# Stored orders and slots, a decay column per batch, two norms on VectorE and single q/k blocks in batch 1, in a fused forgetting attention and SwiGLU kernel

## The chip, the core and the metric

The kernel runs on one core of a Trainium2 chip. A core has five engines that run side by side, each with its own queue of instructions in a fixed order: TensorE (PE, matmuls; PEld is its weight load), VectorE (DVE), ScalarE (ACT), GpSimd (POOL) and SyncE (SP, which here only issues DMAs). Engines wait for each other by semaphores. The metric is the device time of one execution in microseconds (us); before the change it is 378.13 us, the median of three runs (377.17 to 379.72).

## The reference

```python
# q, k, v: (8 batches, 8 heads, 576, 64); f: (8, 8, 576)
scores = np.matmul(q, k.transpose(0, 1, 3, 2)) / np.sqrt(D)
cum = np.cumsum(np.log(np.clip(f, 0.0001, 1.0)), axis=-1)
decay = cum[:, :, :, None] - cum[:, :, None, :]
scores = np.where(causal, -1e9, scores + decay)      # causal: strictly above the diagonal
attn = softmax(scores)                                # max subtracted, exp, divided by the sum
x = np.matmul(attn, v)                                # -> x: (4608 tokens, 512), heads side by side
xn = x / np.sqrt(np.mean(x * x, -1) + 1e-6) * rms_g
g, val = xn @ w_gate, xn @ w_val                      # 512 -> 1536
out = (g * sigmoid(g) * val) @ w_out                  # 1536 -> 512
```

## The kernel before

**Attention.** The sequence of 576 is cut into blocks of 128 rows: blocks 0 to 3 and a last block of 64 (index 4, `LAST`). q and k are loaded with a cast to bf16 and turned, so that the head dimension lies on the partitions (`QT`, `KT`). In batches 0 and 1 TensorE turns blocks 0 to 3 (`turn_pe`, lines 454 to 482); everything else is turned by a DMA from SP's queue (`turn`, line 445). TensorE's turning comes in two forms: single blocks, loaded into `qk` (`load_qk`, line 345), with four transposes and a copy of 512 columns for each of q and k; and pairs of blocks, loaded with rows 2p and 2p+1 in partition p into `qk2` (`load_qk2`, line 356), which is a part of the tile `wt`, with sixteen half-width transposes and a copy of 1024 columns. VectorE copies q and ScalarE copies k out of PSUM. Before the change pairs begin at (batch 0, block 1), (1, 0) and (1, 2); blocks (0, 0) and (0, 3) are single.

The decay is not added to the scores: exp(-cum) of the key multiplies v (`scale_v`, line 487: one multiplication of 128x512 on line 495), and the same factor is written as a 65th column of each head's v (line 496, 128x8), so that the product of the exponentials with this column is the softmax's denominator. The rows' own decay cancels. Batches 0 and 1 are scaled on VectorE, batches 2 to 7 on GpSimd, with one instruction of each kind per block.

Scores (line 520) go through ScalarE's exponential (line 538) into `PT`; GpSimd masks the diagonal blocks (line 545). TensorE multiplies with v (line 564), and VectorE divides by the denominator (lines 578 and 580) into `x`.

**Norm.** `norm` (line 587) squares and sums a block on ScalarE (line 596), takes the power -1/2 on GpSimd (lines 600 and 601), and multiplies on ScalarE (line 608). In batch 0 each block has a norm of its own; later two blocks share GpSimd's part. The result is turned by TensorE for groups 0 and 1 (line 616), by DMA for the others.

**SwiGLU.** Tokens come in nine groups of 512: group b holds blocks 0 to 3 of batch b, and the ninth the eight last blocks. `gate` multiplies with the two weights (line 675) and takes the gate by ScalarE's tanh (line 687) and two VectorE instructions (689 and 682). Groups 0 and 1 work in pieces of 128 tokens, the others in 512. The norm's weights `rms_g` multiply group 0's tokens (line 624), and then, once group 0 has used a third of the gate weights, the weights themselves on VectorE (`weigh`, line 387, instruction on line 393: 24 in all). `project` multiplies with w_out in seven products instead of eight (line 729), with sums of quarter blocks before it (lines 705 to 714), sums of the weights once (line 413), and sums of products after it (line 739).

**What sets the order.** The code first builds a list of units (`Plan.add`): an engine, an expected duration, a function that issues the unit's instructions, the units it depends on, and the buffers (`Hold`, a place in a ring) that it takes and gives back. `Plan.run` (line 119) then plays the list through a small simulation at build time: each engine takes, of its units that are ready and whose buffers are free, the one with the lowest key. The keys come from the string `ORDER`, two characters per unit in the order of adding. Instructions are issued in the order of this simulation, so each engine's queue is fixed; on the chip semaphores hold each instruction until its inputs and its buffer are ready.

Loads of q, k, v and weights are issued from GpSimd's queue (v of block (0, 0), f and `rms_g` from SP's). Lines named below: 298 builds the identity matrix on GpSimd, 351 and 374 issue loads, 479 copies turned q and k.

Of the kernel before, what the change touches and what calls it, by code (L numbers as in the profile page):

```python
# [12 lines left out]
ALU = mybir.AluOpType  # L13
# [3 lines left out]


XPE, DT1, WIDE1 = 2, 0, 0
BASE = -18.8  # L20
VA, NA = 1, 1.2
LETTERS = string.digits + string.ascii_letters
ORDER = (
    "0e1q020d000b0c080j0406030i0a0u0w0l0m0q0r0x090o0E0H0I070p010h050g0f0t0k0y0n0J0s0O0v0T0F1b0K1e0A0W0P1h"
    "0X1u151S1a241y2p2S3o3l44111I1k2g1Z2U1L2E1U2K2d2Z1B2z2n392O3k3s4q323K3h3Z2M3j5s6a373P3w4r404Q3C4z2v3d"
    "3U4J484Y4i59585N4B5m5w6h6O72555G4w5g7c7p4P5y5i627A7M5d5T5L6n7m7B5S6A5X6J7E7Q6Z7d9w9L8l8D828q7T8k8H8Z"
    "8W9c7J7V8P969M9Z7O869C9SaLaWb8boaOb2cHcUcMd2cBcQbpbNaGaPbdbyaUb9bjbDb0bhbubTcectbWcaeoeDeteMexeUe8el"
    "edeqeieAeFf1ePfceHf8hXigifiziliJi3iphSi7iCiPgXh8h1hegPgZhahrh6hkgUh3hphChIhUhshJjijzj7jljCjNjejsjtjG"
    "jHjRkIkTkEkPkNkVlhlFl1lelllTl9lul7lqldly0z0C0B0D0M0G0N0S0L0Q0R0V0U131d191f141i1r1l1s1x1F17181j1z1v1C"
    "1G1N1W27222820262D2L3a2V2T343c2Y383g3u3G2N3p3A3H3v3N3S424c3x4a4j4e4t4x4H4W3I4b4A50454S525b5v5D5F4f4G"  # L30
    "3z3W7g5I5U5P5Y6365474s4L5a6G4Z5t3r3F6x666k6r6e5h5K5r67756s6z6S6K6U71767h5J6C6B7i7t7f8a818o8v8Q9a606V"
    "5B6q8591989i9q9ya25R6Q6j788z6b6X6L7x9g9E9K9R9N7e7U777L8b9Ua1a5a4adaiaoaB7v8ja9aj9oaSaZbabqbEbxbO8J8Y"
    "8T9h9WbMbXc5c7ccck9A9O8f8wataeaq8y8OamcrcEcScybfbwbIc4bGdgdldAdxdKdOdRdVdfdsdndzd4dYebe4eCeKeRf0c6cq"
    "b4bkc0eZf7fdfGfLfPbsbVbZcldhcgcucLcYdofSfXg2g1eVflf6frfgg6gfgkgbgmgqgtgyeyeNeJf5eSgEgHgMh4hhhwhKfhfx"
    "fEfRfohWi2ieirixiHiBiViRj6iZiLj2iqiEjojKjPjVjThohEhyhPhgk2kdkik7kpktkvkyhOi5hHhZhzkBkMkHlvlClSlXhYij"
    "i8iwismcmjmpmsmxmBjSkfjAk1k0jMkajZkjk8mJmVn2mOl8lkkYlalrn9ninnnenrnwnznCm1mdlzlMm9nOnTnVocojoLoQlRm5"
    "lJm0lOp0p6papgpipm0Y100Z121m1o1p1A1M1O1P1T2l2q2r2w3m3t3L3Q464m4l4y4K4R4O535E5M5V646c6i6m6u7I7P7S808e"
    "8i8n8u8A8G8I8N8S8V979f9m9u9s9zaaafaganaQaVaXb1b3bbbibnbBbHbKbQcFcNcOcTd5dcdddidDdIdLdPefejeIeOeWf2f4"
    "fbfefjfufzfWfZgageggglhbhfhjhmhqhxi1i6iaidiiiniGiMiTj1jbjklmlsltlxlAlElLlQlZm4mkmomrmumvmCmQmUmWn0nN"
    "nQogokooosoIoMoZp5p4pbpcpjphpnpqpupPpT161c1g1n1t1K1Q1V1Y211X232f2C2G2A2H2Q2X336E7W8h8r8K3Y4E4I4T5157"  # L40
    "4X545l5f696f6t6M6T6o6v6D878s8F939l8B8X949d9j9x9n9t9G9r9D9I9Va3ac9T9Ya7auc8chcxcKb5brbAbPcpcDbJbRcfc1"
    "cXd0d9dudEd6dbdkdpdvdCdFdMdUeYfafkfqfCfpfyfKftfDfJfTg0g9fOfUg4gjgpgxgAgJhnhDi9iDiYjdiojhjyitiQiUj5jn"
    "jJj0j8jjjqjxjDjEk6lHlWm6mamfmqmhmmmwmAmFmImMmPmYmTmXn6n5n8nbnfnoomoRoUp2p9pkoYp3pdpfpppspwpApFpzpEpJ"
    "pWq0q4q9qh1w1E1D1H1J252c2a2e2k2P3E2W313M4h4v4o4D4M4p5c1R2o2b2h2u292i2j2m2s353f3b3e3n3i3y3q3B3T3D6F2t"
    "2I2y2B2R2x302F2J363R43494d4k3J3V3O3X4g707G5e5A5k5u5H5p615z5W6l747n7a7r7y6H6Y6P6W7b5j795q5x7k7N8g7Y89"
# [31 lines left out]
class Plan:  # L77
# [3 lines left out]
    def __init__(self, rings, fifo):  # L81
        self.units, self.fifo = [], fifo
        self.free = {name: list(range(n)) for name, n in rings.items()}
        self.left = {name: [] for name in rings}

    def add(self, eng, dur, key, emit, deps=(), take=(), give=(), lat=0.04):
        u = Unit(eng, dur, key, emit, lat)
        for h in take:
            if h not in self.left[h.ring]:
                self.left[h.ring].append(h)  # L90
# [96 lines left out]
def fox_ffn_kernel(ctx, tc, q, k, v, f, moe_w_gate, moe_w_val, moe_w_out, moe_rms_g, out):  # L187
# [134 lines left out]
    EARLY = 3  # L322
# [516 lines left out]
```

## Time and profile before

| | |
|---|---|
| median of three runs | 378.13 us (377.17 to 379.72) |
| the profiled execution: device time, span | 376.9 us, 375.2 us |
| TensorE's granted clock, mean | 0.997 |
| busy: PE, DVE, ACT, POOL | 348.3, 290.9, 225.9, 207.5 us |
| weight loads (PEld) | 244.9 us |
| data moved by DMA | 44.87 MB in 133479 packets |

The span runs from the first to the last instruction; the device time has a little around it. Busy times are of one engine, and engines overlap. A row of a timeline or of a group begins with the engine and the line of the kernel, then the operation and its output and inputs; `x24` is a count. A wait is told as "engine line <- engine line that ended it: us in total, times, longest". Rows of a stage begin with the stretch and its length. An instruction's duration runs until it has finished, so a stretched one has stood still for a part of it.

### The profile page before, as it was taken

To read this page: it belongs to the slowest core of one execution; us is meant where nothing else is said; L and a number is where in the kernel's file an instruction comes from. 1 tells how busy PE (TensorE), PEld (TensorE's weight loads), DVE (VectorE), ACT (ScalarE), POOL (GpSimd) and SP (SyncE) were. 2 spreads that over 40 slices of the span, in tenths; PEclk is the share of its full clock that TensorE was granted. 3 is DMA by queue.
4 is the path that set the end of the run, shared out by engine and by line. 5 is a ranking of instruction groups with operands and counts; after the bars stand their busy time and mean duration, and the time that the engine had idled before them with its cause. 6 is when DMAs were issued, how large, how long until landed. Compare 5 with 4: busy or idle time off the path is not lost. (4 is left out here: it accounts for less than half of the span.)

```text
span 375.2 us, 10418 instructions
## 1 busy us (share of the span) xinstructions
PE 348.3 (93%) x4266; PEld 244.9 (65%) x4266; DVE 290.9 (78%) x542; ACT 225.9 (60%) x360; POOL 207.5 (55%) x280
## 2 busy tenths in 40 slices
PE   1799887988999999999999998999999999999994
PEld 1689876978987557755545676556646694445683
DVE  5578997999884868677588887787876976889673
ACT  5696667772897786568957645478833735333210
POOL 8986856899898996775497775842300210000000
PEclk9999999999999999999999999999999999999998
DMA  9999999999999999299199995993201132000015
GB/s 145 214 201 229 181 146 151 168 126 223 170 113 169 185 168 128 67 204 114 33 144 120 162 175 135 143 158 54 40 27 45 41 95 85 0 0 2 28 64 133
DMA packets 133479, 44.87 MB, mean 120 GB/s; under 512 B 117300, under 2 KB 131128, under 8 KB 133432
## 3 DMA queue, kind: packets, MB, share of 16 engines
q0 software_dynamic: 76368, 23.34, 60.7%
q1 hardware_dynamic: 57064, 20.87, 33.1%
q8 instruction: 33, 0.54, 0.6%
q14 instruction: 14, 0.11, 0.1%
HBM read 37.90 MB, written 9.44 MB: 126 GB/s over the span
## 5 line engine op out<-in xcount | busy, mean ns | idle before, releaser
L687 ACT ACTIVATE th<-ff 128x512 f32<-128x512 f32 x108 | 63.9, 596 | 75.8 <-PE ff L675 73.9
L538 ACT ACTIVATE PT<-sc 128x1024 bf16<-128x1024 f32 x96 | 94.8, 1019 | 18.3 <-PE sc L520 16.1
L675 PE MATMUL ff<-xT,wg 128*128 128x128 bf16 (+1 forms) x672 | 96.2, 289 | 3.0 <-DVE hT L682 1.6
L675 PE MATMUL ff<-xT,wv 128*128 128x128 bf16 (+1 forms) x672 | 96.4, 288 | 2.3 <-DVE ores L739 1.2
L689 DVE SCALAR_TENSOR_TENSOR ga<-th,ff 128x512 f32<-128x512 f32 x108 | 73.5, 684 | 25.9 <-ACT th L687 22.4
L682 DVE SCALAR_TENSOR_TENSOR hT<-ga,ff 128x512 bf16<-128x512 f32 x108 | 72.8, 684 | 15.5 <-PE ff L675 13.8
L675 PEld LDWEIGHTS <-wg 128*128 128x128 bf16 x720 | 54.0, 98 | 36.3 <-issue 3.1
L675 PEld LDWEIGHTS <-wv 128*128 128x128 bf16 x720 | 52.8, 98 | 36.3 <-issue 2.5
L545 POOL TENSOR_SCALAR_AFFINE_SELECT PT<-PT 128x1024 bf16<-128x1024 bf16 x32 | 36.0, 1124 | 52.7 <-ACT PT L538 52.6
L729 PEld LDWEIGHTS <-hT 128*128 128x128 bf16 x432 | 41.4, 98 | 7.3 <-issue 0.2
L564 PEld LDWEIGHTS <-PT 128*128 128x128 bf16 x896 | 38.0, 99 | 11.5 <-issue 1.6
L564 PE MATMUL ff<-Vs,PT 128*128 128x65 bf16 x896 | 42.3, 195 | 2.1 <-POOL PT L545 0.7
L739 DVE TENSOR_TENSOR ores<-ores,ff 128x512 f32<-128x512 f32 x45 | 30.6, 684 | 17.0 <-PE ff L729 12.9
L729 PE MATMUL ff<-wo,hT 128*128 128x256 bf16 x324 | 39.5, 273 | 0.0
L495 POOL TENSOR_TENSOR Vs<-v,decT 128x512 bf16<-128x512 f32 (+1 forms) x30 | 31.7, 1057 | 10.2 <-DMA v<-in_v_dram 6.6
L520 PE MATMUL sc<-QT,KT 64*128 64x128 bf16 (+1 forms) x960 | 34.1, 213 | 2.3 <-ACT PT L538 1.7
L580 DVE TENSOR_TENSOR x<-ff,rden 128x256 f32<-128x256 f32 (+1 forms) x80 | 33.8, 423 | 2.8
L608 ACT ACTIVATE xn<-x,rs 128x512 bf16<-128x512 f32 (+1 forms) x40 | 27.8, 719 | 13.0 <-POOL rs L601 12.9
L374 POOL DMA_DIRECT2D v<-in_v_dram x39 | 34.6, 888 | 1.8 <-DVE hT L682 1.0
L729 PEld LDWEIGHTS <-sm 128*128 128x128 bf16 x324 | 30.9, 98 | 6.7 <-issue 2.0
L520 PEld LDWEIGHTS <-KT 64*128 64x128 bf16 x960 | 24.5, 96 | 14.4 <-issue 12.5
L351 POOL DMA_DIRECT2D qk<-in_k_dram x34 | 29.6, 879 | 4.5 <-DMA wo<-in_moe_w_out_dram 3.4
(74 smaller groups left out, 351.7 us busy)
## 6 DMA issues: line engine op xcount, KB each, us to landing
out_dram<-ores SPq DMA_DIRECT2D x32, 256.0 KB, 2.6
v<-in_v_dram POOLq DMA_DIRECT2D x31, 256.0 KB, 6.6
qk<-in_k_dram POOLq DMA_DIRECT2D x26, 128.0 KB, 6.7
qk<-in_q_dram POOLq DMA_DIRECT2D x26, 128.0 KB, 6.0
wg<-in_moe_w_gate_dram POOLq DMA_DIRECT2D x3, 512.0 KB, 10.7
wv<-in_moe_w_val_dram POOLq DMA_DIRECT2D x3, 512.0 KB, 13.1
wo<-in_moe_w_out_dram POOLq DMA_DIRECT2D x2, 768.0 KB, 12.1
v<-in_v_dram POOLq DMA_DIRECT2D x8, 128.0 KB, 6.8
```

The source lines that it names most:

```text
L374: queue.dma_start(out=T_v32[h.slot][0:n, :, :], in_=v[b, :, p0:p0 + n, :].rearrange("h p d -> p h d"))
L495: eng.tensor_tensor(T_Vs[hv.slot][0:n, j, :, 0:D], T_v32[h.slot][0:n, :, :], bcast(dj, D), ALU.mult)
L520: nc.tensor.matmul(t[:, par, c:c + n], lhsT=kt[r, p, kj * 128:(kj + 1) * 128], rhs=qt[r, p, qi * 128:qi * 128 + n], start=True, stop=True)
L538: nc.scalar.activation(T_of_p[hp.slot][:, 0:2 * half].rearrange("p (a c) -> p a c", a=2)[:, :, 0:cols], T_sc[h.slot][:, :, 0:cols], ACT.Ex ...
L545: nc.gpsimd.affine_select(out=d, in_=d, pattern=[[0, 8], [1, n]], compare_op=ALU.is_ge, fill=0.0, base=0, channel_multiplier=-1)
L564: nc.tensor.matmul(po[:, p, :], lhsT=T_of_p[h.slot][:, c:c + 128], rhs=vs[:, kj, 2 * p + par, :], start=(kj == 0), stop=(kj == qi))
L580: nc.vector.tensor_tensor(d, po[:, :, 0:D], bcast(r, D), ALU.mult)
L675: nc.tensor.matmul(T_ff[h.slot][:, c:c + n], lhsT=w[:, dc, fc * 128:(fc + 1) * 128], rhs=xT[:, dc, t0:t0 + n], start=(dc == 0), stop=(dc = ...
L682: nc.vector.scalar_tensor_tensor(hT, in0=three[0], scalar=0.5, in1=three[1], op0=ALU.mult, op1=ALU.mult)
L687: th = act(0.6, key - 0.1, lambda: nc.scalar.activation(T_th[ht.slot], T_ff[hg.slot], ACT.Tanh, scale=0.5), [ug], take=[ht])
L689: a = dve(0.69, key - 0.1, lambda: nc.vector.scalar_tensor_tensor(T_ga[ha.slot], in0=T_th[ht.slot], scalar=1.0, in1=T_ff[hg.slot], op0=ALU ...
L729: nc.tensor.matmul(t[:, s * HD:(s + 1) * HD], lhsT=a()[:, fc, s * 128:(s + 1) * 128], rhs=w[:, fc, :], start=(not more and s == 0 and fc = ...
```

## The change

- `Plan.run` no longer simulates. `ORDER` is now a full ranking of the units over all engines, and a second string, `SLOTS`, gives each buffer's place in its ring. [...] `run` sorts the units by rank and asserts that dependencies and buffers are respected; which waits an engine has still follows from the order and the slots.
- The decay column (line 496) stays as it was for batch 0. For batches 1 to 7 it is one GpSimd instruction per batch, of 128 partitions by 5 blocks by 8 heads, instead of one per block; the values (line 564) depend on it as well.
- The norms of blocks (0, 0) and (0, 1) have their square with its sum, and their multiplication, on VectorE instead of ScalarE. The power between them stays on GpSimd. The buffer `xn` of these two is taken at the square, whose output goes there.
- Blocks (1, 2) and (1, 3) are loaded and turned as single blocks, not as a pair.
- Some expected durations in the units differ; they no longer have an effect, since nothing is simulated. `COPY_DVE` is empty, and the condition on the gates' width (`g < 2`) gives the same groups as before.

```diff
-XPE, DT1, WIDE1 = 2, 0, 0
+XPE = 2
+PAIRS = {(0, 1), (1, 0)}
+NORM_DVE = {(0, 0), (0, 1)}
+COPY_DVE = set()
 ORDER = (
-    "0e1q020d000b0c080j0406030i0a0u0w0l0m0q0r0x090o0E0H0I070p010h050g0f0t0k0y0n0J0s0O0v0T0F1b0K1e0A0W0P1h"
...
+    "000102030a0j06050b090c070g0h0v0z0o0p0s0t0A0d0l0M0W0U0f0q0i0u040e080k0m0x0D110n0G0y0Y0w0S0N1k0I15101C"
...
+SLOTS = (
+    "12301120000132014372632143570512533110656813567a42470b603923321550723224214461031877302176215a0b5309"
...
     def run(self):
...
+        for h, c in zip(self.holds, SLOTS):
+            h.slot = LETTERS.index(c)
+        ranks = [LETTERS.index(a) * len(LETTERS) + LETTERS.index(b) for a, b in zip(ORDER[::2], ORDER[1::2])]
...
+        order = [u for _, u in sorted(zip(ranks, self.units), key=lambda x: x[0])]
...
     for j in (0, 2):
-        if DT1 * 2 > 3 - j:
+        if (1, j) not in PAIRS:
             for i in (j, j + 1):
                 load_qk(1, i, -9.5 + i * 0.1)
...
         def emit(eng):
...
             eng.tensor_tensor(T_Vs[hv.slot][0:n, j, :, 0:D], T_v32[h.slot][0:n, :, :], bcast(dj, D), ALU.mult)
-            eng.tensor_copy(T_Vs[hv.slot][0:n, j, :, D], dj)
+            if b == 0:
+                eng.tensor_copy(T_Vs[hv.slot][0:n, j, :, D], dj)
...
+        if b > 0 and j == 0:
+            column[b] = pool(0.25, key, lambda: nc.gpsimd.tensor_copy(
+                T_Vs[hv.slot][:, :, :, D], decT[:, :, b * H:(b + 1) * H]), [L_dec], take=[hv])
+        scaled[b, j] = us + [column[b]] if b > 0 else us
...
     def norm(b, js, key):
...
+                if on_dve:
+                    nc.vector.scalar_tensor_tensor(T_xn[hn.slot][0:n, :], in0=x, scalar=1.0, in1=x, op0=ALU.mult,
+                                                   op1=ALU.mult, accum_out=sq[:, i:i + 1])
+                    return
...
-                nc.scalar.mul(T_xn[hn.slot][0:n, :], T_x[hx.slot][0:n, :], rs[:, i:i + 1])
+                mul = nc.vector.tensor_scalar_mul if on_dve else nc.scalar.mul
+                mul(T_xn[hn.slot][0:n, :], T_x[hx.slot][0:n, :], rs[:, i:i + 1])
...
-        if b >= 2 or qi == LAST or (b == 1 and qi >= 4 - 2 * DT1):
+        if b >= 2 or qi == LAST:
             turn(b, qi, qkey(b, qi) - 0.25)
-        elif (b, qi) in {(0, 0), (0, 1), (0, 3), (1, 0), (1, 2)}:
-            turn_pe(b, qi, (b, qi) in {(0, 1), (1, 0), (1, 2)}, qkey(b, qi) - 0.25)
+        elif (b, qi - 1) not in PAIRS:
+            turn_pe(b, qi, (b, qi) in PAIRS, qkey(b, qi) - 0.25)
```

More of the change, by code (lines that the diff above doesn't have):

```diff
@@ L77, with __init__ @@
 class Plan:
[L81 to L84, printed above, removed]
+    def __init__(self, rings):
+        self.units, self.rings, self.holds = [], rings, []
     def add(self, eng, dur, key, emit, deps=(), take=(), give=(), lat=0.04):
@@ L489, in scale_v @@
         h, hv = hold_v[b, j], hold_Vs[b]
+        early = b == 0 and j < EARLY
         def emit(eng):
```

223 lines of the change are left out of this document (90 added, 133 removed).

## The prediction

> **What bounds the kernel now.** I read the page first, then the engines' busy time by stage, then what TensorE waited for, then single lines where the stage named an engine.
>
> ```profile
> span 375.2 us, 10418 instructions
> ...
> PE   1799887988999999999999998999999999999994
> ...
> PE 39%; DVE 2%; issue 0%; DVEq 0%
> ```
>
> The chain of waits that ended last covers only the final 41% of the span and is nearly all TensorE (39%); the slices of PE show dents in the first ten slices (some 100 us) and again near the 24th. So late work is matmul after matmul, and what can be won lies early. Busy time by stage says where:
>
> ```profile
> core 0: us, PE busy (x) PEld busy (x) DVE busy (x) ACT busy (x) POOL busy (x), PEclk, DMA share, GB/s
> 0.00:10.00 10.00, 2.27 (x22) 1.97 (x22) 5.02 (x25) 4.81 (x6) 8.80 (x17) 1.00 1.23 151
> 10.00:30.00 20.00, 17.24 (x295) 15.09 (x292) 13.33 (x31) 17.16 (x25) 17.43 (x23) 1.00 1.41 205
> 30.00:110.00 80.00, 71.22 (x1396) 65.93 (x1393) 74.47 (x147) 53.38 (x83) 63.66 (x83) 1.00 1.57 169
> 110.00:200.00 90.00, 89.34 (x1013) 54.52 (x1012) 65.26 (x127) 68.34 (x111) 69.14 (x93) 1.00 1.15 135
> 200.00:240.00 40.00, 38.26 (x418) 26.04 (x416) 31.82 (x47) 22.84 (x36) 31.50 (x41) 1.00 1.18 147
> 240.00:360.00 120.00, 120.00 (x1046) 72.63 (x1045) 93.90 (x161) 58.20 (x99) 17.00 (x27) 1.00 0.26 51
> 360.00:375.20 15.20, 9.96 (x92) 8.68 (x89) 7.14 (x10) 1.17 (x2) 0.00 (x0) 0.92 0.39 104
> ```
>
> TensorE's idle time, stage by stage (length less PE busy): 7.73 before 10 us, 2.76 to 30, 8.78 to 110, 0.66 to 200, 1.74 to 240, none to 360, 5.24 in the tail. The first is mostly loads and the tail is the last sum and its store; neither is work the change takes away. What a better order can reach is 2.76 + 8.78 + 0.66 + 1.74 = 13.9 us. From 30 to 110 us VectorE is busy 74.47 of 80, more than any other engine: it is the bound there. From 10 to 30 ScalarE (17.16) and GpSimd (17.43) are the busy ones and VectorE has 6.67 free. TensorE's waits agree:
>
> ```profile
> PE ff L464 <- DVE ident L299: 7.7, 1, 7.7
> PE ff L616 <- ACT xn L608: 2.7, 3, 2.3
> PE ff L675 <- DVE hT L682: 2.2, 3, 0.9
> PE sc L520 <- ACT PT L538: 1.7, 2, 1.3
> ```
>
> After the first matmul the longest are on ScalarE's norm and exponentials, then on VectorE's gate outputs.
>
> **The change part by part.** *1. Order and the shared port.* The columns of the first two rows are shortest/median/longest ns:
>
> ```profile
> L393 DVE TENSOR_SCALAR wg<-wg,rgT x12: 330/350/1760, 45.9 to 86.3; 128x512 bf16<-128x512 bf16 x12
> L393 DVE TENSOR_SCALAR wv<-wv,rgT x12: 334/437/2286, 63.5 to 92.8; 128x512 bf16<-128x512 bf16 x12
> ```
> ```profile
> 30.00:110.00 80.00, 13.33 (x24) 1.00 1.57 169
> ```
> ```profile
> 79.27 0.98 POOL L374 DMA_DIRECT2D v<-in_v_dram  x1
> 80.26 1.11 POOL L545 TENSOR_SCALAR_AFFINE_SELECT PT<-PT 128x1024 bf16<-128x1024 bf16 x1
> ...
> 78.13 3.61 DVE L393 TENSOR_SCALAR wv<-wv,rgT 128x512 bf16<-128x512 bf16 x3
> ```
>
> The 24 weight scalings of line 393 took 13.33 us, all inside the bound stage. At the shortest, 0.33, they would take 7.9: 5.4 us are stretch. Three of them fill 3.61 us where 1.0 would do, and GpSimd works all through it (the issue at 79.27, the mask from 80.26). The other stretched line there is the scaling of v:
>
> ```profile
> L495 DVE TENSOR_TENSOR Vs<-v,decT x7: 683/692/2281, 19.9 to 87.1; 128x512 bf16<-128x512 f32 x5, 64x512 bf16<-64x512 f32 x2
> ```
> ```profile
> 30.00:110.00 80.00, 6.96 (x6) 9.54 (x9) 1.00 1.57 169
> ```
>
> Six took 6.96 us (first busy column); six medians are 4.15, so 2.8 are stretch. Together 8.2 us of the bound engine in its stage. The stored order can win between nothing and all of it. I take two thirds, 5.5: the medians of line 393 (0.35, 0.44) show that half of them run unstretched already, so there is room to place them.
>
> [...]
>
> *2. Decay column.*
>
> ```profile
> L496 POOL CAST Vs<-decT x30: 208/221/982, 77.8 to 252.1; 128x8 bf16<-128x8 f32 x24, 64x8 bf16<-64x8 f32 x6
> L496 DVE CAST Vs<-decT x7: 173/181/368, 20.5 to 88.1; 128x8 bf16<-128x8 f32 x5, 64x8 bf16<-64x8 f32 x2
> ```
>
> Five casts of batch 1 leave VectorE: 5 x 0.18 = 0.9 us. On GpSimd 30 casts go and 7 come, of 40 elements instead of 8; between 0.21 and 0.98 each by the row, nearer 0.22 as the size hardly shows there. GpSimd is not TensorE's wait, so I count nothing for that. The new column instruction waits for the batch's Vs buffer, and behind it in GpSimd's queue stand load issues; but the scaling of block 0 has waited for the same buffer at the same place, except in batch 1, whose buffer is free from the start.
>
> *3. Single blocks in batch 1.*
>
> ```profile
> L479 DVE COPY QT<-ff x5: 414/1284/1302, 8.3 to 42.3; 128x1024 bf16<-128x1024 bf16 x3, 128x512 bf16<-128x512 bf16 x2
> ```
> ```profile
> L351 POOL DMA_DIRECT2D qk<-in_k_dram x34: 687/906/1099, 1.3 to 237.5; - x34
> ```
>
> One copy of 1.30 becomes two of 0.41 on VectorE: 0.5 less, and ScalarE's K copy likewise. TensorE's 32 half-width transposes become 16 full ones, which I count as equal. Two loads become four: two more issues, 1.8 us on GpSimd's queue, with the last loads of batches 0 and 1 and the output weights behind them. GpSimd is free 16.3 us in that stage, so between 0 and +1.8; I take +0.2.
>
> VectorE thus gets 5.5 + 0.9 + 0.5 = 6.9 us back between 30 and 110. TensorE cannot get back more than its 8.78 idle, and some VectorE time freed will stand as VectorE idle (5.53 already does); at four fifths the term is -5.5.
>
> *4. Two norms on VectorE.*
>
> ```profile
> L689 DVE SCALAR_TENSOR_TENSOR ga<-th,ff 128x512 f32<-128x512 f32 x108 | 73.5, 684 | 25.9 <-ACT th L687 22.4
> ...
> L608 ACT ACTIVATE xn<-x,rs 128x512 bf16<-128x512 f32 x32 | 22.0, 720 | 7.4 <-POOL rs L601 7.2
> L596 ACT ACTIVATE junk<-x 128x512 bf16<-128x512 f32 x32 | 20.2, 631 | 6.1 <-DVE x L580 5.9
> ```
>
> ScalarE loses 2 x (0.63 + 0.72) = 2.7 us between 10 and 30, where it is nearly full. VectorE gains two squares (0.68 by line 689, the same operation) and two multiplies, shown nowhere: between 0.33 (line 393 in 16 bit) and 0.72 (line 608); I take 0.45, the input being twice as wide as line 393's. That is 2.3 us, in the 6.67 that VectorE has free, so nothing if the wait for GpSimd's power lies beside other work (rival C if it doesn't). TensorE's idle there is 2.76, and the waits on line 608 and on the exponentials, 4.4 us over the run, belong largely to this stage. I take -1.0, between 0 and -2.76.
>
> *5. The first loads.* Two characters in the stored string are a unit's rank, in the order in which units are added. The issues of q and k of block (0,0) are units 26 and 28, that of the pair's q is unit 32. Their keys were 07, 01 and 0f; their ranks are now 0f, 0i and 08. So GpSimd issues the pair's q first, then q, then k; before it was k, q, pair.
>
> ```profile
> 1.31 1.10 POOL L351 DMA_DIRECT2D qk<-in_k_dram  x1 [0.81 <-POOLq L823]
> 2.41 0.90 POOL L351 DMA_DIRECT2D qk<-in_q_dram  x1
> ```
> ```profile
> 9.59 0.61 PE L520 MATMUL sc<-QT,KT 64*128 64x128 bf16 x8
> ```
> ```profile
> DMA to landing us min/median/max: 4.0/5.1/7.8
> ```
>
> k goes out 1.10 + 0.90 = 2.0 us later, at 3.31, and lands (third row: time to landing of these loads before 10 us) between 7.3 and 11.1; with transposes and copy, about 1 us, the first scores could begin anywhere from no later than now, 9.59, to 12.1: +0 to +2.5. Against that the identity, made on GpSimd by line 298, now comes behind five load issues instead of six, 0.9 earlier, and TensorE's first wait, 7.7, was for it: -0.5 at best. I take +0.3, near the short end, since the pair's transposes fill the time.
>
> *6. 200 to 240 us.*
>
> ```profile
> L708 DVE TENSOR_TENSOR hT<-hT x9: 945/953/1832, 70.1 to 361.3; 128x1536 bf16<-128x1536 bf16 x9
> ```
>
> The sums of the seven-product scheme stretch from 0.95 to as much as 1.83, and TensorE's idle is 1.74. I take -0.8, between 0 and -1.7.
>
> Everything else (slots stored instead of handed out by the planner, the planner's own durations) issues no instruction. Sum: -5.5 - 1.0 - 0.8 + 0.2 + 0.3 = -6.8 us. The profiled execution took 376.9 us (span 375.2 and 1.7 around it), so it would take 370.1; the median of the runs is 378.13, 1.2 above, and the forecast is for such a median: 378.1 - 6.8 = **371.3**.
>
> **The rivals.** A difference under 1% (3.8 us) can't be told from none.
>
> *B, no change.* The stretch moves instead of going: GpSimd is busy 63.66 and VectorE 74.47 of the same 80 us, so their sum is 138, and they must overlap for at least 58 us whatever the order. Many VectorE instructions are never stretched (line 689's mean of 684 hardly leaves room), which speaks against it; that GpSimd's loads cannot wait speaks for it. Then parts 2 to 5 alone remain: four fifths of 1.4, the 1.0 of the norms, less 0.5, so -1.6 and 376.5.
>
> *C, slower.* The norms' multiplies now stand in VectorE's queue waiting for GpSimd's power, and what is queued behind them (evacuation of attention values, copies of Q, gates) waits too, and TensorE and ScalarE with it.
>
> ```profile
> ACT xn L608 <- POOL rs L601: 12.9, 10, 2.5
> ```
>
> ScalarE lost up to 2.5 us in one such wait. Two of them on VectorE are 5.0 us between 10 and 30, passed on whole if nothing else was placed between square and multiply; it decides once the two exceed VectorE's slack at that point. With the port's gain eaten: 378.1 + 5.0 = 383. Against it: the free 6.67.
>
> *D, the loads held up.* If the two multiplies keep GpSimd from issuing, its queue, 17.43 of 20 us full, slips by up to 2 x 0.72 = 1.4 and the norms' gain of 1.0 is lost: 371.3 + 2.4 = 373.7. No issue in the row of line 351 was stretched past 1.10, though line 393 ran beside many, so the trace speaks against it.
>
> [...]
>
> **How the numbers follow.** Forecast 0.55, B 0.25, C 0.13, D 0.07. The forecast's bounds: at best all 13.9 us of reachable idle less a little, 378.1 - 13.6 = 364.5; at the other end, a third of the port's gain and k late by 2.5 gives about 376. The range 364.5 to 380 leaves out most of C and a few per cent on the fast side. Faster by over 1% means under 374.3: forecast and D, 0.62. Within 1%: B, 0.25. Slower: C, 0.13.
>
> **What would show it.** Line 393's 24 scalings near 8 to 9 us instead of 13.33, and line 495 on VectorE near 0.69 each. TensorE's idle between 30 and 110 at 3 to 4 us instead of 8.78. Line 608's share on VectorE, with a wait on GpSimd's power well under 1 us; a wait of 2 would mean C. First scores between 9 and 10.5 us. The forecast is wrong if line 393 is short and TensorE's idle stays: then another engine was the bound.

## The result, and the profile after

Measured side by side, the changed kernel takes 0.9866 of the time of the kernel before, with a 95% interval of 0.9825 to 0.9907: 378.13 x 0.9866 = 373.1 us, where 371.3 was forecast. The comparison takes only executions within 1.5% of the fastest of the same kernel, which here are 7 of 20 of the changed kernel and all 20 of the kernel before; over all 20 the medians are 379.42 us after and 379.61 before. So the changed kernel reaches the gain in a part of its executions only, and its median shows none: it runs from 372.64 to 383.74 us, the kernel before from 377.03 to 382.26.

Two executions of the changed kernel were profiled. The first took 378.31 us, the second 373.24. This is the page of the second, in the order of the lines shown of before (the span; busy time by engine; the slices of TensorE, its granted clock and DMA; the chain of waits):

```profile
span 371.5 us, 10375 instructions
...
PE 346.8 (93%) x4250; PEld 244.2 (66%) x4250; DVE 282.9 (76%) x544; ACT 223.7 (60%) x355; POOL 205.8 (55%) x259
...
PE   0789988799999999999999999999999999999993
...
PEclk9969999999999999999999999999999999999999
DMA  9999999999999999399999954991100341000024
...
PE 85%; POOL 6%; DVE 4%; issue 2%; ACT 2%; POOLq 0%; DVEq 0%; ACTq 0%
```

The dents near the 24th slice are gone, those in the first ten are not, and the clock row has a 6 that was not there before. Busy time by stage, same execution (columns as in the prediction):

```profile
0.00:10.00 10.00, 1.13 (x12) 1.04 (x14) 5.13 (x23) 4.31 (x6) 8.79 (x15) 1.00 1.30 155
10.00:30.00 20.00, 16.18 (x274) 13.91 (x271) 15.28 (x37) 13.46 (x16) 18.28 (x24) 0.83 1.34 216
30.00:110.00 80.00, 74.15 (x1454) 69.00 (x1452) 69.90 (x144) 56.35 (x92) 63.52 (x80) 1.00 1.65 163
110.00:200.00 90.00, 89.78 (x1021) 54.40 (x1019) 65.65 (x130) 70.04 (x112) 77.00 (x94) 1.00 1.29 154
200.00:240.00 40.00, 40.00 (x422) 27.73 (x420) 30.36 (x54) 21.59 (x35) 21.52 (x27) 1.00 0.86 130
240.00:360.00 120.00, 120.00 (x1033) 73.33 (x1032) 93.10 (x155) 57.38 (x96) 16.74 (x23) 1.00 0.22 48
360.00:371.50 11.50, 5.59 (x52) 4.77 (x49) 3.44 (x5) 0.58 (x1) 0.00 (x0) 0.97 0.39 92
```

TensorE's idle time (length less PE busy), beside that of before and the forecast:

| stage | before | after | difference | forecast |
|---|---|---|---|---|
| 0 to 10 | 7.73 | 8.87 | +1.1 | +0.3 (first loads) |
| 10 to 30 | 2.76 | 3.82 | +1.1 | -1.0 (norms) |
| 30 to 110 | 8.78 | 5.85 | -2.9 | -5.3 (port, column, blocks) |
| 110 to 200 | 0.66 | 0.22 | -0.4 | 0 |
| 200 to 240 | 1.74 | 0.00 | -1.7 | -0.8 (sums) |
| after 360 | 5.24 | 5.91 | +0.7 | 0 |
| TensorE's busy time | 348.3 | 346.8 | -1.5 | 0 |
| span | 375.2 | 371.5 | -3.7 | -6.8 |

So two stages gave time and the first 30 us took some back. Idle time does not hold what a lower clock costs: in the first profile, of span 376.6 us, sixteen score matmuls of one shape (line 482) take 1.04 us from 22.14 us on, at a granted clock of 0.50, and 0.62 us from 26.51 on, at 1.00. The stage from 10 to 30 us has a clock of 0.83, and in the second profile 274 matmuls, where before it had 1.00 and 295. The first profile, 5.1 us longer, has the same start and loses most of the rest in one place:

```profile
span 376.6 us, 10345 instructions
```
```profile
30.00:110.00 80.00, 71.25 (x1354) 66.11 (x1350) 71.00 (x136) 52.17 (x83) 58.77 (x74) 0.98 1.59 162
```

There TensorE is idle 8.75 us between 30 and 110, as before the change (8.78).

**The scalings and GpSimd.** The 24 weight scalings (now line 347), first in the execution of 371.5, then in that of 376.6; shortest/median/longest ns, and all 24 in the stage as the first busy column:

```profile
L347 DVE TENSOR_SCALAR wg<-wg,rgT x12: 333/345/1627, 43.4 to 82.6; 128x512 bf16<-128x512 bf16 x12
L347 DVE TENSOR_SCALAR wv<-wv,rgT x12: 333/344/765, 58.0 to 88.7; 128x512 bf16<-128x512 bf16 x12
```
```profile
30.00:110.00 80.00, 9.95 (x24) 1.00 1.65 163
```
```profile
L347 DVE TENSOR_SCALAR wg<-wg,rgT x12: 334/344/2122, 43.4 to 81.0; 128x512 bf16<-128x512 bf16 x12
L347 DVE TENSOR_SCALAR wv<-wv,rgT x12: 333/346/3980, 57.9 to 89.4; 128x512 bf16<-128x512 bf16 x12
```
```profile
30.00:110.00 80.00, 15.48 (x24) 0.98 1.59 162
```

13.33 us became 9.95 in the one and 15.48 in the other. The long one of 3.98 us is seen in the timeline of VectorE and GpSimd (start, length), and TensorE's longest waits of that execution say who paid:

```profile
86.72 6.65 DVE L347 TENSOR_SCALAR wv<-wv,rgT 128x512 bf16<-128x512 bf16 x3
...
88.21 2.16 POOL L453 TENSOR_TENSOR Vs<-v,decT 128x512 bf16<-128x512 f32 x2
90.31 0.93 POOL L328 DMA_DIRECT2D v<-in_v_dram  x1
91.24 0.90 POOL L305 DMA_DIRECT2D qk<-in_k_dram  x1
92.13 1.08 POOL L453 TENSOR_TENSOR Vs<-v,decT 64x512 bf16<-64x512 f32 x1
93.13 0.46 POOL L460 CAST Vs<-decT 128x40 bf16<-128x40 f32 x1
```
```profile
PE ff L646 <- DVE wv L347: 4.4, 2, 3.7
```

Three scalings fill 6.65 us where 1.0 would do. The last starts at 89.4 and ends at 93.4; from 89.2 to 93.2 GpSimd runs four instructions in a row (a scaling of v, two issues of loads, a scaling of v) and then begins a fifth. TensorE waits 3.7 us for it. In the execution of 371.5 no wait of TensorE on line 347 is listed. The stall costs more than itself, by windows of the first profile (the number after the five busy columns is the granted clock):

```profile
90.00:92.00 2.00, 0.00 (x0) 0.00 (x0) 2.00 (x1) 0.00 (x0) 2.00 (x3) 1.00 1.01 186
92.00:94.00 2.00, 0.57 (x9) 0.58 (x10) 2.00 (x3) 0.00 (x0) 2.00 (x4) 0.96 1.09 178
94.00:96.00 2.00, 2.00 (x21) 2.00 (x20) 1.79 (x3) 0.60 (x1) 2.00 (x3) 0.50 0.79 47
96.00:98.00 2.00, 2.00 (x28) 2.00 (x26) 0.84 (x2) 0.22 (x1) 2.00 (x3) 0.68 1.27 89
98.00:100.00 2.00, 2.00 (x40) 2.00 (x38) 1.29 (x2) 0.81 (x2) 2.00 (x4) 1.00 1.66 112
```

For some 4 us the clock is at 0.50 to 0.68, and TensorE, busy throughout with matmuls of one shape (line 646), does 21 and 28 where 40 go from 98 us on, at 1.00. Just before that it did next to nothing, from 89.8 to 93.4. Between 10 and 30 us of the same kernel the clock is lower too (0.83 over the stage), with a longest gap of TensorE there of 1.55 us in this execution and 1.66 in that of 371.5; what lowers it there isn't shown.

The other operations counted as stretched went as hoped: the scaling of v on VectorE (line 453) and the sums (line 679), both from the execution of 371.5:

```profile
L453 DVE TENSOR_TENSOR Vs<-v,decT x7: 676/685/1033, 22.4 to 74.3; 128x512 bf16<-128x512 f32 x5, 64x512 bf16<-64x512 f32 x2
...
L679 DVE TENSOR_TENSOR hT<-hT x9: 941/948/952, 67.4 to 358.0; 128x1536 bf16<-128x1536 bf16 x9
```

The longest were 2.28 and 1.83 us before, and are 1.03 and 0.95 now.

**The start.** Timeline of the changed kernel (execution of 371.5), and below it the same two first lines of an experiment that sets the first loads' order back (it is told below):

```profile
6.97 1.35 DVE L263 TENSOR_TENSOR_SCAN hT<-one,hT 64x576 f32<-64x576 f32 x1 [0.67 <-ACT hT L257]
7.10 1.31 POOL masks.py:199 TENSOR_SCALAR_AFFINE_SELECT ident_f<-ident_f 128x128 f32<-128x128 f32 x1
...
8.87 1.01 PE L418 MATMUL ff<-ident,qk 128*128 128x128 bf16 x8 [8.87 <-DVE ident L253]
...
10.81 0.61 PE L482 MATMUL sc<-QT,KT 64*128 64x128 bf16 x8
```
```profile
5.19 1.35 DVE L263 TENSOR_TENSOR_SCAN hT<-one,hT 64x576 f32<-64x576 f32 x1 [0.67 <-ACT hT L257]
...
7.09 0.29 POOL masks.py:199 TENSOR_SCALAR_AFFINE_SELECT ident_f<-ident_f 128x128 f32<-128x128 f32 x1
```

The stored order issues v before f on SP's queue. So the scan over f comes 1.8 us later and meets GpSimd's instruction that makes the identity, which takes 1.31 us instead of 0.29. TensorE's first matmul starts at 8.87 instead of 7.73, the first scores at 10.81 instead of 9.59. How much the order of the loads costs differs between executions: in six experiments with the same first loads the scan starts between 6.08 and 6.32, the instruction that it meets takes 0.42 to 0.55 us, and the first matmul starts at 7.98 to 8.22. Between 10 and 30 the granted clock is 0.83, where it was 1.00; the late start alone is not shown to be the cause, since of two of those experiments the one that starts at 8.22 (the column per block) keeps 1.00 and the one that starts at 7.98 (the norms on ScalarE) has 0.83.

**The norms.** Multiplication on VectorE, and what it waited for between 10 and 30 us, execution of 376.6:

```profile
L579 DVE TENSOR_SCALAR xn<-x,rs x2: 486/512/537, 21.0 to 24.6; 128x512 bf16<-128x512 f32 x2
```

```profile
DVE xn L579 <- POOL rs L571: 0.6, 1, 0.6
```

It took 0.51 us (0.45 was assumed), and only one of the two waited for GpSimd's power, 0.6 us.

### The profile page after: what moved, and what is told of

It reads as the page before. It is cut to its first block, busy times and chain, and to the rows that moved or that the text cites. A ratio compares the mean times of both kernels' runs of the same rounds, so it can differ in the third digit from the quotient of the medians.

```text
span 376.6 us, 10345 instructions
## 1 busy us (share of the span) xinstructions
PE 348.2 (92%) x4220; PEld 246.6 (65%) x4250; DVE 288.2 (77%) x544; ACT 224.0 (59%) x355; POOL 206.5 (55%) x259
## 2 busy tenths in 40 slices
DMA packets 135561, 44.88 MB, mean 119 GB/s; under 512 B 119381, under 2 KB 133209, under 8 KB 135513
## 4 chain that ended last, share of the span: by engine, by line
PE 79%; POOL 7%; DVE 5%; DMA 4%; issue 3%; ACT 1%; POOLq 0%; ACTq 0%; DVEq 0%
PE ff L646 44%; PE ff L700 20%; PE ff L526 8%; PE sc L482 6%; DMA qk<-in_k_dram 4%; DVE wv L347 2%; POOL PT L507 2%; POOL qk L305 1%; DVE ga L660 1%; ACT PT L500 1%; POOL wt L317 1%; DVE x L542 1%; POOL v L328 1%; POOL Vs L453 0%; POOL rs L571 0%
## 5 line engine op out<-in xcount | busy, mean ns | idle before, releaser
L646 PE MATMUL ff<-xT,wg 128*128 128x128 bf16 (+1 forms) x655 | 95.1, 289 | 0.6
L646 PEld LDWEIGHTS <-wv 128*128 128x128 bf16 x720 | 54.6, 99 | 40.6 <-DVE wv L347 4.7
L507 POOL TENSOR_SCALAR_AFFINE_SELECT PT<-PT 128x1024 bf16<-128x1024 bf16 x32 | 39.1, 1222 | 53.9 <-ACT PT L500 50.7
L579 ACT ACTIVATE xn<-x,rs 128x512 bf16<-128x512 f32 (+1 forms) x38 | 26.3, 718 | 11.2 <-POOL rs L571 11.2
L305 POOL DMA_DIRECT2D qk<-in_q_dram x36 | 31.3, 871 | 0.0
```

What stands on the lines that cost most here:

```text
L305: nc.gpsimd.dma_start(out=T_qk[h.slot][0:n, :].rearrange("p (h d) -> p h d", d=D), in_=src[b, :, p0:p0 + n, :].rearrange("h p d -> p h d"))
L507: nc.gpsimd.affine_select(out=d, in_=d, pattern=[[0, 8], [1, n]], compare_op=ALU.is_ge, fill=0.0, base=0, channel_multiplier=-1)
L646: nc.tensor.matmul(T_ff[h.slot][:, c:c + n], lhsT=w[:, dc, fc * 128:(fc + 1) * 128], rhs=xT[:, dc, t0:t0 + n], start=(dc == 0), stop=(dc = ...
```

## The experiments

The theory after the result: the gain comes from the stored order and slots; it is smaller than forecast since VectorE's busy time between 30 and 110 us is worth less than the four fifths assumed; and where it is absent, a weight scaling is held by GpSimd (the port theory of the expectations: the runs show the holding, and none shows a port). The rivals: VectorE is the bound and the stretch alone decides; the late start decides; the norms or the column took the gain back. Ratios are to the kernel before, run in turn on the same chip, with 95% intervals.

**The same kernel again.** No edit.

> The changed kernel unaltered, for its own spread and for comparison with the three beside it. Its 20 executions so far lie between 372.64 and 383.74 us. Port theory: the spread is made by where GpSimd's instructions happen to fall against the weight scalings of line 347; so this profile again shows one or more scalings far above their shortest 0.33 us, and TensorE waits on line 347 by about the same amount. Rival (late data, or the granted clock): the 24 scalings add up to much the same whatever the time, and the slower executions show a lower clock or later landings.

0.9885 (0.9812 to 0.9958), six executions from 373.24 to 383.24 us. The result stands, and so does the spread. The profile of 371.5 above is from here: a short execution, in which TensorE doesn't wait on the scalings. Their sum, 9.95 us against 15.48 in the long one, is not the same whatever the time, as the rival had it.

**Kernel before, without the weight scalings.**

```diff
-                    nc.vector.tensor_scalar_mul(w[:, dc, c0:c1], w[:, dc, c0:c1], rgT[:, dc:dc + 1])
+                    pass
```

> The kernel before with the 24 weight scalings of line 393 left out, so that the gate products use weights without rms_g for groups 1 to 8; nothing else differs. VectorE loses 13.33 us of its 74.47 between 30 and 110 us. This measures the conversion that the forecast set at four fifths. If VectorE is the bound of that stage as forecast, four fifths of 13.33 is more than the 8.78 us that TensorE is idle there, so nearly all of the idle would go: idle at about 1 us, time 379 - 8 = 371. If the planner's fixed order and the loads set the end as well (rival: the freed time stands as VectorE idle), idle falls by less than half: 5 or more stays, and the time is 375 or above.

1.0014 (0.9974 to 1.0053), median 379.74 us. 13.33 us of work leave VectorE, and the time does not move. The conversion of four fifths falls, and with it the reading that VectorE is the bound of this stage. Where the freed time went isn't known: the execution that was profiled took 1239 us, for reasons its trace doesn't show, and says nothing on this. The kernel leaves out the norm's weights for groups 1 to 8.

**Kernel before, weight scalings on ScalarE.**

```diff
-                    nc.vector.tensor_scalar_mul(w[:, dc, c0:c1], w[:, dc, c0:c1], rgT[:, dc:dc + 1])
-            Lw[nm, i] = [dve(2.0, key, emit, deps[nm])]
+                    nc.scalar.mul(w[:, dc, c0:c1], w[:, dc, c0:c1], rgT[:, dc:dc + 1])
+            Lw[nm, i] = [act(2.0, key, emit, deps[nm])]
```

> The same move in the kernel before the change (planner and all else as before): what the stretched scalings cost there. Port theory, as the prediction had it: 5.4 us of stretch and 7.9 us of work leave the engine that bounds the stage from 30 to 110 us, so 3 to 6 us less, 372 to 376. Rival (the stretch was hidden, or ScalarE becomes the bound): within 1.5 us of the kernel before.

1.0057 (1.0023 to 1.009). Its stage row:

```profile
30.00:110.00 80.00, 72.17 (x1362) 64.88 (x1360) 60.41 (x119) 66.11 (x106) 59.49 (x79) 0.98 1.75 165
```

VectorE fell from 74.47 to 60.41 us, and TensorE's idle from 8.78 to 7.83 only: 14 us for 1. ScalarE took on 13 us in exchange, so this alone would not be clean; with the experiment above it says the same. TensorE's longest waits of this stage are now 2.8 us for a gate output of VectorE and 2.4 for GpSimd's mask: as one wait went, others came.

**Changed kernel, weight scalings on ScalarE.** The same edit.

> The 24 weight scalings of the changed kernel are made on ScalarE, in the same place of the global order. [...] Port theory: about 24 x 0.7 = 17 us more on ScalarE, VectorE freed of 8 to 15 us, no stretch, time 370 to 374 and spread under 4 us. Rival: ScalarE's exponentials and gates are delayed by 1.5 to 3 us at each of the six groups and TensorE waits for them instead: no faster than the changed kernel, 376 to 382.

1.0146 (1.0089 to 1.0203), the slowest of all. TensorE's longest waits between 10 and 110 us:

```profile
PE sc L482 <- ACT PT L500: 5.8, 4, 3.0
PE ff L418 <- ACT KT L436: 3.9, 1, 3.9
```

None of the 24 is stretched on ScalarE (707 to 722 ns). But a fixed order made for other engines doesn't bear such a move: the exponentials and the copy of K now stand behind the scalings, for which the stored order had left no place.

**Changed kernel, weight scalings in a form that also writes a sum.** The same product, plus zero, with its sum written to a spare column:

```diff
-                    nc.vector.tensor_scalar_mul(w[:, dc, c0:c1], w[:, dc, c0:c1], rgT[:, dc:dc + 1])
+                    nc.vector.tensor_scalar(w[:, dc, c0:c1], in0=w[:, dc, c0:c1], scalar1=rgT[:, dc:dc + 1],
+                                            op0=ALU.mult, scalar2=0.0, op1=ALU.add, accum_out=spare[:, 0:1])
```

> The 24 weight scalings stay on VectorE in the same places, but as an instruction that also writes a sum (to a spare column), which by the port theory does not take the port shared with GpSimd. Port theory: each takes 0.6 to 0.7 us, none is stretched beyond 0.8, so 24 take 14 to 16 us, TensorE's wait on this line (4.4 us in the profile of the changed kernel) goes below 1, and the times lie between 371 and 376 with a spread under 4 us. Rival: GpSimd is not what holds them; the extra 6 us of work on VectorE (0.25 more for each) come on top, 380 or more, and the spread stays.

0.9968 (0.9939 to 0.9997); all 12 executions between 375.55 and 380.38 us.

```profile
L348 DVE TENSOR_SCALAR_CACHE_REDUCE wg<-wg,rgT x12: 729/746/747, 42.6 to 83.0; 128x512 bf16<-128x512 bf16 x12
...
L348 DVE TENSOR_SCALAR_CACHE_REDUCE wv<-wv,rgT x12: 728/746/747, 58.5 to 90.7; 128x512 bf16<-128x512 bf16 x12
```
```profile
30.00:110.00 80.00, 71.69 (x1390) 66.59 (x1387) 73.52 (x164) 54.45 (x86) 62.28 (x77) 1.00 1.67 164
```

None of the 24 is stretched in this profile. The last four run one after the other from 88.30 to 91.40 us beside the same row of GpSimd instructions (88.14 to 93.32) that held line 347 for 3.98 us: what stretches line 347 goes with GpSimd's instructions and with the form of the scaling (3.98 us in the one, 0.73 to 0.75 in the other), and not with its inputs or its queue; by what way GpSimd holds it isn't shown. The price is 0.75 instead of 0.34 us, and 0.08 for reading the sum, which begins just before the scaling ends. The 24 scalings with their 24 readings:

```profile
30.00:110.00 80.00, 18.03 (x48) 1.00 1.67 164
```

That is 8.1 us more than the 9.95 of the execution of 371.5, for a span 2.3 us longer. By these two executions 1 us of VectorE was worth about 0.3; by the ratios (0.9968 against 0.9866, 3.9 us) about 0.5. The times that the port theory gave (371 to 376 us) did not come: without the stretch, but with the dearer form, the short times are nearly gone, and so are those above 380.4.

**Only two of the six groups of scalings in that form,** those that were stretched most, the first third of wg and the last of wv (3.1 and 6.9 us for four in the execution of 376.6, where the four from 57.92 us on take 1.1):

```diff
+ONE_PORT = {("g", 0), ("v", 2)}
...
+                    if (nm, i) in ONE_PORT:
+                        nc.vector.tensor_scalar(w[:, dc, c0:c1], in0=w[:, dc, c0:c1], scalar1=rgT[:, dc:dc + 1],
+                                                op0=ALU.mult, scalar2=0.0, op1=ALU.add, accum_out=spare[:, 0:1])
+                        continue
```

> [...] Port theory: the slower group of times (378 to 384) goes, the faster (372 to 377) stays: 372 to 377 for nearly all runs, ratio to the kernel before 0.985 to 0.99. Rival: the slower times come from elsewhere (landings, clock): about 6 in 10 runs stay above 378.

0.9846 (0.9798 to 0.9895): 371.66, 372.63, 373.31, 374.38, 375.71 and 382.54 us. By ratio this can't be told from the changed kernel; what differs is how often the short time is reached: five of six executions here lie under 376 us, against 6 of the 20 first ones of the changed kernel and 1 of the 6 above. The case of 382.54 us shows another stall, told below.

**The first loads in the old order.** The ranks of the loads of f and of the first v are exchanged:

```diff
-    "000102030a0j06050b090c070g0h0v0z0o0p0s0t0A0d0l0M0W0U0f0q0i0u040e080k0m0x0D110n0G0y0Y0w0S0N1k0I15101C"
+    "00010203040j06050b090c070g0h0v0z0o0p0s0t0A0d0l0M0W0U0f0q0i0u0a0e080k0m0x0D110n0G0y0Y0w0S0N1k0I15101C"
```

> In the changed kernel SP issues the load of f ahead of that of v's first block again, as the kernel before did; two ranks are swapped, nothing else. Port theory for the start: the scan (line 263, two inputs in the on-chip memory) then ends before GpSimd builds the identity, the mask of line masks.py:199 takes 0.3 us instead of 1.31, and TensorE starts at about 8.2 us (when q has landed) instead of 8.87. Rival: the identity is late because GpSimd issues six loads ahead of it, whatever VectorE does; TensorE starts at 8.8 again. The end moves by 0.7 us at most, which the times can't show; the profile of the first 10 us decides.

The first matmul is back at 7.70 us and the clock between 10 and 30 at 1.00 (17.68 us busy instead of 16.18). Yet the ratio is 1.0022 (0.998 to 1.0064). The row of line 347 names what met it:

```profile
L347 DVE TENSOR_SCALAR wv<-wv,rgT x12: 333/346/3978, 55.6 to 93.1; 128x512 bf16<-128x512 bf16 x12
```

The long stall is there again, in an execution of 378.92 us, shorter than this kernel's median of 380.44. The earlier start isn't shown to be its cause: such a stall stands in the execution of 376.6 too, and in two experiments below (3.98 us with the norms on ScalarE, 3.00 with order, slots and single blocks alone), and all three start later.

**Both: the old first loads, and two groups in the form with the sum.**

> [...] Port theory: f ahead alone was in the slower group of times in all 12 runs, and its profile has the value weights' last third held for 3.98 us in one instruction; with that group off the port the earlier start is kept: 370 to 375 in nearly all runs, ratio to the kernel before 0.978 to 0.987. Rival: the earlier start shifts TensorE into later instruction fetches or other waits, as f ahead alone did: 376 or more.

0.9886 (0.9848 to 0.9924), median 376.73 us; 11 of 12 executions lie under 378.3. Against the kernel with the first loads alone (1.0022) that is 1.4% less (1.0% by the medians of all 12 of each), with the form of the two groups the only difference: what the stall of the scalings costs that kernel is thereby shown. But against two groups alone (0.9846) the earlier start adds nothing. In its profile:

```profile
PE ff L532 <- issue: 2.9, 1, 2.9
```
```profile
30.00:110.00 80.00, 73.44 (x1392) 67.96 (x1390) 69.80 (x147) 54.79 (x87) 61.11 (x76) 0.98 1.84 164
```

Of the 2.7 us of idle time won ahead of 30 us against the execution of 371.5, 0.7 comes back before 110 (6.56 us of idle, 2.9 of it in one gap that waits for no engine); and TensorE's busy time is 3.4 us longer (350.2), with the clock at 0.98 over that stage, where it was 1.00 in the execution of 371.5.

**The norms back on ScalarE.**

```diff
-                if on_dve:
-                    nc.vector.scalar_tensor_tensor(T_xn[hn.slot][0:n, :], in0=x, scalar=1.0, in1=x, op0=ALU.mult, ...
-            us.append((dve if on_dve else act)(0.73, key, emit, [evac[b, j, 0], evac[b, j, 1]],
+            us.append(act(0.73, key, emit, [evac[b, j, 0], evac[b, j, 1]],
...
-                mul = nc.vector.tensor_scalar_mul if on_dve else nc.scalar.mul
+                mul = nc.scalar.mul
```

> The changed kernel with the two norms of batch 0 back on ScalarE (squares and multiplies at the same ranks). Forecast's reasoning: 1.0 us slower, with TensorE busy about 1 us less between 10 and 30. Rival C: up to 5 us faster, if VectorE stood waiting for GpSimd's power. The profiles so far show VectorE waiting 0.6 us for it, and TensorE idle 3.0 us between 10 and 30, no less than before the change; so I expect within 1 us of the changed kernel.

0.9832 (0.9777 to 0.9887): no slower than with them on VectorE. The term of 1.0 us isn't there.

**The decay column per block again.**

```diff
-            if b == 0:
+            if True:
                 eng.tensor_copy(T_Vs[hv.slot][0:n, j, :, D], dj)
...
-            column[b] = pool(0.25, key, lambda: nc.gpsimd.tensor_copy(
-                T_Vs[hv.slot][:, :, :, D], decT[:, :, b * H:(b + 1) * H]), [L_dec], take=[hv])
+            column[b] = pool(0.25, key, lambda: None, [L_dec], take=[hv])
```

> The changed kernel with the decay column written per block again (after each scaling of v, on its engine); the instruction per batch is left out. Forecast's reasoning: 5 x 0.18 us more on VectorE in batch 1 and 24 more casts on GpSimd, so 0.7 us slower, not to be told by the times. Port theory: the casts lie in GpSimd's chains that hold VectorE's scalings and sums, so stretches come back (line 347 above 10 us, sums of lines 676 to 685 above 1.2 us each), 1 to 4 us slower than the changed kernel.

0.9895 (0.984 to 0.9949): the same within the intervals. In its profile the scalings of line 347 take 11.19 us, one of them 2.94, but TensorE doesn't wait on them. So the stretches that the port theory expected came back in small part, and in this execution without a price.

**Order, slots and single blocks alone:** both edits above together.

> The changed kernel with the norms back on ScalarE and the decay column per block: what is left of the change is the stored order, the slots, and the single blocks of batch 1. Each part undone alone gave fast times of 371.9 to 375.2, no slower than the changed kernel's 372.6 to 376.8. If order and slots carry the gain: fast times 372 to 376, ratio 0.983 to 0.992 to the kernel before. If the two parts matter together (as the forecast's 1.0 + 0.7 us): 374 to 378, ratio 0.99 to 0.997.

0.9885 (0.9831 to 0.9939). Order, slots and single blocks carry the whole gain that can be measured; no run separates the three. The two other parts may even do harm: of the last three kernels' executions 10 of 18 lie under 376 us, of the changed kernel's 7 of 26, which is too few to tell.

**Longer packets.** q, k and v of batches 2 to 7 are read as one run of 2 KB per partition instead of eight pieces (the same number of bytes, but not the rows that attention needs); the edit for v, that for q and k is alike:

```diff
+            if b >= 2:
+                flat_in = v[b].rearrange("h s d -> (h s d)")[p0 * 512:(p0 + n) * 512]
+                queue.dma_start(out=T_v32[h.slot][0:n, :, :].rearrange("p h d -> p (h d)"),
+                                in_=flat_in.rearrange("(p c) -> p c", c=512))
+                return
```

> In the changed kernel the loads of q, k and v of batches 2 to 7 read the same number of bytes as one run of 2 KB for each partition instead of eight runs of 256 bytes, so that the DMA engines have an eighth of the packets there; what is read is not what attention needs from batch 2 on, all other work stays. Fetch theory: TensorE's gaps that end by nothing in the profile (near 61.6 us 1.3 to 2.5, near 68.6 us 0.8 to 2.5, in one profile 5.4 near 87) are its own instructions, 16 KB at a time, coming late behind those packets; with fewer packets each of these gaps falls below 0.5 us and TensorE's idle time between 30 and 110 falls by 2 to 4 us. Rival: the gaps have nothing to do with the DMA load and stay above 1 us. For the stretched scalings: if GpSimd's issues get shorter with fewer packets the stretch falls as well; if they stay near 0.9 us the stretch stays.

This tests the gaps that wait for nothing the profile shows. In the execution of 371.5 there are two between 30 and 110 us; TensorE's timeline, and the DMA queues while the first of them began (60 to 62 us):

```profile
63.15 0.25 PE L526 MATMUL ff<-Vs,PT 128*128 128x65 bf16 x3 [1.52 <-issue]
...
70.99 1.25 PE L700 MATMUL ff<-wt,sm 128*128 128x256 bf16 x10 [2.19 <-issue]
```
```profile
q8 instruction: 1, 0.02, 4.0%
```

A packet of instructions, one of 33 of 16 KB in the run, is on its way from 60.6 to 61.9 just as the first gap begins (61.6), and from 68.6 to 69.5 in the second (68.8 to 71.0). In the 382.54 us case above the gap is 5.4 us (87.1 to 92.4), and its packet takes 1.9 us, from 88.7 to 90.6. Before the change the longest gap of this kind between 30 and 110 was 0.5 us. With long packets (87,176 instead of 135,561, the bytes being the same) the ratio is 0.976 (0.9696 to 0.9823), four executions from 369.16 to 376.72 us, and the gap near 69 us is gone; but one of 4.0 us stays near 62. So fewer packets seem to help, by about 1% beside 0.9866, with a ratio that rests on two executions. TensorE's idle between 30 and 110 us hardly moved (5.53 instead of 5.85), though the 24 scalings took only 8.53 us there. The edit also shortens the issues on GpSimd, from 0.90 to 0.56 us each, and no run changes the fetch by itself.

What the traces add: over the 13 profiles other than that of 1239 us TensorE has 26 gaps of 0.4 us or more between 30 and 110 us that wait for nothing shown, and 24 of them end 1.2 to 1.8 us after one of these packets has arrived, though the packets come some 7 us apart. So the gaps follow the arrival of these packets. The kernel before has as many packets (33) and one such gap, of 0.5 us; why there are more after the change isn't shown. Side by side, the profiled executions by time (those with the scalings on VectorE; all between 30 and 110 us; a dash: the scalings are of two forms):

| us | kernel | the 24 scalings | TensorE's waits on them | its gaps that wait for nothing |
|---|---|---|---|---|
| 376.90 | before | 13.33 | none listed | 0.5 |
| 373.24 | changed | 9.95 | none listed | 3.7 |
| 374.71 | old first loads and two groups | - | 0.8 | 3.5 |
| 375.09 | column per block | 11.19 | none listed | 3.6 |
| 375.55 | form with the sum | 18.03 with readings | 0.8 | 0.7 |
| 375.67 | long packets | 8.53 | none listed | 4.0 |
| 378.31 | changed | 15.48 | 4.4 | 2.3 |
| 378.92 | old first loads | 16.13 | 4.1 | 4.6 |
| 381.64 | norms on ScalarE | 15.61 | 4.4 | 5.5 |
| 382.49 | order alone | 14.86 | 1.9 | 7.1 |
| 382.54 | two groups | - | none listed | 9.0 |

So the stretched scalings are one part of what makes an execution long, and the gaps are the other; in the three longest the gaps are the greater part, and four of the five shortest after the change lose 3.5 us or more to them, where the kernel before lost 0.5. The one without these gaps pays for the dearer scalings.

## Why the prediction was right and where it was wrong

By the ratio the side, the size to 1.8 us (371.3 against 373.1) and the range held. But the forecast was for a median of runs, and the median of all 20 is 379.42 us, where rival B (376.5, no change) stood nearer; and the spans of the two executions laid side by side differ by 3.7 us, about half of the 6.8. The working behind the number held only in parts.

- **Part 1, the size of the stretch: partly.** "Two thirds" of 8.2 us were to go. In the execution of 371.5, line 347 fell by 3.4 us and line 453 from 6.96 to 3.9, so 6.5 us went. In that of 376.6 line 347 rose by 2.2. The sign by which to read this, "8 to 9 us", was met in neither (9.95 and 15.48). No run shows the shared port that this part is named for; what the runs showed is that scalings of the plain form are held beside GpSimd's instructions, one of them for 3.98 us, and those that also write a sum are not (0.73 to 0.75 us each).
- **Part 1 to 3, what freed VectorE time is worth: wrong.** "It is the bound there" and "at four fifths" is the step that failed. 13.33 us taken away brought nothing, 14 us moved to ScalarE brought 1 of TensorE's idle and a longer time, 8.1 us added cost 2.3 to 3.9: between nothing and half a us for each. The view that I read for it, the busy share, doesn't say who ends TensorE's waits, and the list of waits taken by stage is only half a warning: between 30 and 110 us the longest was on ScalarE's norm, 2.5 us, but VectorE ended 5.7 of the 8.7 listed. Only leaving the work out showed its worth.
- **Part 2, the column: free,** as counted for GpSimd; the 0.9 on VectorE isn't seen.
- **Part 4, norms: wrong.** The durations were right (0.68 and 0.51 us), the gain of 1.0 wasn't there. The reason given for it was misread: of the 4.4 us of waits on the norm and the exponentials that "belong largely to this stage", 1.9 lay between 10 and 30 us, and of the norm's 2.7 only 0.2; a wait of 2.3 ends at 62.7. By stage, kernel before, 10 to 30 and then 30 to 110 us:

```profile
PE ff L616 <- ACT xn L608: 0.2, 1, 0.2
```
```profile
PE ff L616 <- ACT xn L608: 2.5, 2, 2.3
```

  After the change TensorE waits 0.9 us between 10 and 30 for the norm that VectorE now makes. Rival C's waits of 2.5 us came to one of 0.6.
- **Part 5, first loads: mis-sized.** +0.3 was forecast for the order of k, q and the pair; +1.1 came in the two profiled executions (+0.25 to +0.5 in the six experiments named above), from a place that I had not looked at: SP's queue, where v now stands before f, and through f the scan beside which GpSimd's identity took 1.31 us instead of 0.29. The bounds (to +2.5) hold it. Undoing it brought no time.
- **Part 6, sums: right place, mis-sized:** -1.7 instead of -0.8, which is all of the idle there. It is the one term whose mechanism and place were both seen as argued.
- **Rival B** ("the stretch moves instead of going") describes the execution of 376.6: two kinds of operation are free of it, and one scaling takes 3.98 us. I had given it one price for all executions; in fact the same program does either.
- **A term that the sum lacks:** TensorE's gaps that wait for nothing, 0.5 us before between 30 and 110 us, are 2.3 and 3.7 in the two executions of the changed kernel.
- **Rival D** is seen in small: beside the multiplication at 21.00 us an issue took 1.18 us, where the median of its line is 0.92. That is 0.26 of the 1.4 that D counted.
- **The sum.** Within 30 to 110 us -2.9 stands for -5.3; the sums' extra 0.9, TensorE's busy time (-1.5, not forecast) and 110 to 200 us (-0.4) made good a part of it, and the start (+0.8 over its term), the norms (+2.1 in their stage) and the end (+0.7) took more. That the total came near was in part such balancing, so in part luck.

What stays open: what sets the time of the stage from 30 to 110 us. Neither VectorE's load nor the start does alone. The fetch of instructions beside a busy DMA is the candidate, as the gaps follow its packets (24 of 26), the DMA slices stand at 9 there and fewer packets brought time; but the DMA slices stood at 9 before the change too, and no run separates the fetch from the loads' landing and GpSimd's issues.

## What to carry to other kernels

A high busy share marks an engine worth looking at, not one whose time is worth anything: before pricing freed time, leave the work out and see whether the end moves. An order stored ahead of the run is only as good as the chip's repeatability: here one program ran with its scalings at 9.95 us and at 15.48. An instruction that must never stand in the way may be better put in a form that the profile doesn't show held (here 0.75 us with the sum, against 0.34 to 3.98 without), and only that one, as the form has its price (with two groups of six, five of six executions took the short time; with all six groups, one of twelve). Look also at idle time that no engine ends: it was as large as the stall that the experiments were after. Whoever reorders loads should follow each queue to the first thing that needs its data.

## What the runs showed that I had not expected

- A weight scaling on VectorE stood through several GpSimd instructions in a row: 3.98 us, four of them, two of them DMA issues. It did not get on when the first of them ended.
- One stall of 3.7 us cost more than itself, as the granted clock was 0.50 to 0.68 in the next 4 us: 49 matmuls, where 80 of the same shape go at 1.00.
- TensorE's gaps that wait for no engine end 1.2 to 1.8 us after a packet of instructions has arrived, in 24 of 26 cases; one lasted 5.4 us.
- The scalings that also write their sum were not stretched (728 to 747 ns, 24 times), at about twice the time of a plain one that nothing holds (344 ns).
